# Low bits of the weights: from an OR on VectorE to an integer add on GpSimd

## Chip, cores and metric

The kernel runs on one core of one Trainium2 chip. The metric is the device time of one execution in microseconds, as the median of several runs. The names of the engines are those of the profile: PE (TensorE matmul), PEld (its weight loads), DVE (VectorE), ACT (ScalarE), POOL (GpSimd), SP (SyncE, whose queue issues every DMA of this kernel).

## What is computed

A linear attention with exponential features feeds a small feed-forward block.

```python
def phi(x):
    proj = einsum('bhsd,df->bhsf', x, w_phi)
    proj = proj - max(abs(proj), axis=-1)
    return concatenate([exp(proj), exp(-proj)], axis=-1)
q_p, k_p = phi(q), phi(k)                       # q, k, v: 8 x 8 x 576 x 64; 128 features
kv, z = einsum('bhsf,bhsd->bhfd', k_p, v), sum(k_p, axis=2)
x = (q_p @ kv) / (q_p @ z + 1e-6)               # turned to 4608 x 512
h = x @ w_in                                    # w_in 512 x 1024
solu = h * softmax(h)
ln = (solu - mean) / sqrt(var + 1e-6) * g_ln
out = ln @ w_out                                # w_out 1024 x 512
```

The weights come as 64-bit floats, and the kernel makes 32-bit floats of them on the chip, from the high word and the top three bits of the low one.

## The kernel before

The attention is cut into 16 units (batch by half of the heads), the feed-forward block into 36 tiles of 128 tokens. `op` declares some 2460 pieces of work, each with an engine, a function and what it comes after; the long tuple `SEQUENCE` lists their numbers in the order in which they are issued. Each engine works through its own pieces in that order and never passes one by, so a piece that waits holds up all that is behind it on its engine. The order is written out; nothing is decided when the program runs. A tile's buffer slot is given by the same order (`Plan.order`).

In an attention unit PE projects q and k (`qp`, `kp`, `pm`; tiles pjq, pjk, pjm), DVE takes the row maxima (m) and subtracts them (dq, dk), ACT makes the exponentials (fq, ek), PE sums them against v (`K`, `rest`, `Z`, all in tile kvT), and then makes numerators (`qo`, `qr`: num) and denominators (`qd`: den); DVE takes the reciprocal (`dc`), it goes through DRAM to be spread over partitions (rb), and POOL multiplies (`dv`: xa, xb). In a feed-forward tile ACT and POOL split x in a high and a low part (`xh`, `xl`: mxh, mxl), PE makes h from them in 24 matmuls, the softmax parts follow on DVE and ACT, the result is turned through DRAM (du, uTs), split (`uh`, `ul`), and PE makes o in 24 matmuls; ACT scales it (os), and SP stores it.

The weights come in eight pieces of 128 x 1024 pairs of 32-bit words: pieces 0 to 3 are w_in, 4 to 7 are w_out. For each piece i the steps are `wl` (SP loads it, tile wraw, 1 MB), `ws` (ACT changes the exponent of the high word in place), `wb` (two DVE steps in `w_bits`, below: the high word shifted left by 3 into tile w, then the top 3 bits of the low word or-ed in). For w_in `wh` (ACT, win_h) and `wlo` (POOL, win_l) split the result; for w_out `wg` (ACT) multiplies the gain in, `cm`, `cmp`, `cma`, `cms` make the column mean through PE and ACT, and `wc`, `woh`, `wol` subtract it and split. The raw pieces of w_in lie in the buffers of xa and xb: pieces 1 and 3 in xa, 0 and 2 in xb. So piece 3 is loaded only when piece 1 is done, piece 2 when 0 is done, and the first `dv` writes xa when piece 3 is done. The first tile's h (`moe 0 h`) comes after all four `wlo` and its own `xl`.

The profile puts nearly all instructions on L258, the line of a helper that keeps the order, so they are told apart by their tiles.

Of the kernel before, what the change touches and what calls it, by code (L numbers as in the profile page):

```python
# [8 lines left out]
U32 = mybir.dt.uint32  # L9
AF = mybir.ActivationFunctionType  # L10
ALU = mybir.AluOpType
# [14 lines left out]
KV_PE = (0, 1)  # L26
SWITCH = 165.0
# [1285 lines left out]
```

## Time and profile before

| | us |
|---|---|
| median of 3 runs (670.62 to 671.99) | 671.8 |
| the profiled execution: its own time | 670.49 |
| the profiled execution: its span, first to last instruction | 668.7 |
| PE busy | 660.4 (99%) |
| DVE busy | 491.6 (74%) |
| ACT busy | 370.3 (55%) |
| POOL busy | 394.6 (59%) |

The table's busy times are unions of spans over the whole execution. A matmul's end is modelled in the trace and lies some tenths of a microsecond behind its last column, so a PE that reads as busy may still be waiting a little; the distance from one start to the next is the better measure.

### The profile page before, as it was taken

Reading aid. Unit: us, or ns where it says so; the run is one execution under the profiler, and the core shown is the slowest. Engines: PE = TensorE matmul, PEld = TensorE weight load, DVE = VectorE, ACT = ScalarE, POOL = GpSimd, SP = SyncE. Lnnn points to the kernel's source line nnn. Section 1 sums busy time; section 2 is a strip of 40 time slices with the busy share of each in tenths; the row PEclk is TensorE's granted clock in tenths of the full one; section 3 lists DMA queues with packets and bytes.
Section 4 is the critical chain, followed back from the end, with each engine's and each line's share of the span. In section 5 each row is a group of like instructions: output and inputs, shape, how many; then the busy total and the mean of one; then the engine's idle time right before and its main releaser. Section 6 shows DMA issues by size and latency. Waiting matters only on the chain.

```text
span 668.7 us, 13163 instructions
## 1 busy us (share of the span) xinstructions
PE 660.4 (99%) x4932; PEld 493.9 (74%) x4932; DVE 491.6 (74%) x754; ACT 370.3 (55%) x717; POOL 394.6 (59%) x438
## 2 busy tenths in 40 slices
PE   8999999999999999999999999999999899999998
PEld 6776667677777777777768777787777677788887
DVE  6999888878987697797788888589675746533440
ACT  4888874566465565455664576364545563331322
POOL 0125998786675574677593955845857555554501
PEclk9999999999999999999999999999999999999999
DMA  7897888777765695887685667764874663532302
GB/s 269 303 310 230 277 215 237 220 223 243 243 192 185 217 292 191 238 260 221 191 262 158 202 210 215 263 189 124 259 218 144 213 206 92 183 113 85 104 16 80
DMA packets 131280, 135.31 MB, mean 202 GB/s; under 512 B 55568, under 2 KB 105104, under 8 KB 130704
## 3 DMA queue, kind: packets, MB, share of 16 engines
q1 hardware_dynamic: 131216, 134.46, 65.1%
q8 instruction: 39, 0.64, 0.4%
q14 instruction: 25, 0.20, 0.1%
HBM read 85.53 MB, written 48.91 MB: 201 GB/s over the span
## 4 chain that ended last, share of the span: by engine, by line
PE 86%; DVE 9%; DMA 2%; issue 1%; POOL 1%; ACT 0%; SPq 0%; DVEq 0%; POOLq 0%; ACTq 0%
PE o L258 29%; PE h L258 28%; PE kvT L258 11%; PE num L258 6%; PE pjq L258 4%; PE pjk L258 4%; PE den L258 3%; DVE m L258 2%; DVE dq L258 2%; DVE w L258 2%; DVE dk L258 1%; PE pjm L258 1%; DMA out<-os 1%; DMA rb<-d 1%; DVE dE L258 0%
## 5 line engine op out<-in xcount | busy, mean ns | idle before, releaser
L258 POOL TENSOR_TENSOR uls<-uTs,uhs 128x1024 fp32r<-128x1024 f32 x33 | 78.9, 2391 | 46.4 <-ACT uhs L258 34.9
L258 PE MATMUL o<-w_out_h,uhs 128*128 128x512 f32 x264 | 103.9, 393 | 0.0
L258 PE MATMUL o<-w_out_h,uls 128*128 128x512 f32 x264 | 102.8, 389 | 0.0
L258 PE MATMUL o<-w_out_l,uhs 128*128 128x512 f32 x264 | 102.8, 389 | 0.0
L258 ACT ACTIVATE ek<-dk 128x512 f32<-128x512 f32 (+1 forms) x160 | 88.8, 587 | 18.8 <-DVE dk L258 15.5
L258 POOL TENSOR_TENSOR zt<-ek 128x512 f32<-128x512 f32 x52 | 68.2, 1311 | 48.8 <-ACT ek L258 48.3
L258 PE MATMUL h<-win_h,mxh 128*128 128x512 f32 x288 | 91.9, 400 | 0.0
L258 ACT ACTIVATE fq<-pT 128x512 f32<-128x512 f32 (+1 forms) x140 | 74.1, 561 | 31.6 <-DMA pT<-dqd 21.3
L258 PE MATMUL h<-win_h,mxl 128*128 128x512 f32 x288 | 89.0, 390 | 0.5 <-POOL mxl L258 0.5
L258 PE MATMUL h<-win_l,mxh 128*128 128x512 f32 x288 | 89.0, 390 | 0.0
L258 DVE TENSOR_REDUCE nm<-h 128x1 f32<-128x1024 f32 x36 | 43.8, 1218 | 60.0 <-PE h L258 60.0
L258 ACT ACTIVATE eu<-h,nm 128x1024 f32<-128x1024 f32 x36 | 40.1, 1113 | 59.9 <-DVE nm L258 52.3
L258 PEld LDWEIGHTS h<-win_h,mxh 128*128 128x128 f32 x288 | 52.0, 188 | 15.4 <-issue 1.4
L258 PEld LDWEIGHTS h<-win_h,mxl 128*128 128x128 f32 x288 | 54.0, 188 | 12.4 <-POOL mxl L258 0.9
L258 PEld LDWEIGHTS h<-win_l,mxh 128*128 128x128 f32 x288 | 54.1, 188 | 11.6
L258 PE MATMUL kvT<-ek,rawv 128*64 128x256 f32 x512 | 62.0, 383 | 0.0
L258 DVE SCALAR_TENSOR_TENSOR qz<-fq,kvf,qz 128x576 f32<-128x576 f32 x46 | 44.2, 972 | 21.1 <-ACT qz L258 21.1
L258 PEld LDWEIGHTS o<-w_out_h,uhs 128*128 128x128 f32 x264 | 49.6, 188 | 11.7 <-issue 0.5
L258 PEld LDWEIGHTS o<-w_out_h,uls 128*128 128x128 f32 x264 | 49.6, 188 | 10.4
L258 PEld LDWEIGHTS o<-w_out_l,uhs 128*128 128x128 f32 x264 | 49.6, 188 | 10.0
L258 PE MATMUL num<-fq,kvf 128*64 128x448 f32 (+1 forms) x304 | 56.5, 499 | 0.0
L258 ACT ACTIVATE qz<-fq,kvf 128x576 f32<-128x576 f32 x46 | 34.6, 770 | 38.2 <-DMA kvf<-dk 38.2
(109 smaller groups left out, 1278.1 us busy)
## 6 DMA issues: line engine op xcount, KB each, us to landing
du<-ub SPq DMA_DIRECT2D x33, 512.0 KB, 3.9
uTs<-du SPq DMA_DIRECT2D x33, 512.0 KB, 5.2
rb<-d SPq DMA_DIRECT2D x64, 144.0 KB, 3.9
dqd<-dq SPq DMA_DIRECT2D x14, 640.0 KB, 4.9
pT<-dqd SPq DMA_DIRECT2D x14, 640.0 KB, 5.9
out<-os SPq DMA_DIRECT2D x35, 256.0 KB, 4.1
rawq<-in_q SPq DMA_DIRECT2D x32, 256.0 KB, 4.2
rawk<-in_k SPq DMA_DIRECT2D x32, 256.0 KB, 5.0
```

Of the source, the lines that this page charges most:

```text
L258: return self.tc.keep_in_program_order(method(*args, **kwargs))
```

## The change

The second step of `w_bits` is replaced. The three low bits are taken out of the low word in a step of their own, in place (`"lo"`), and are then added to the shifted high word by POOL as a 32-bit integer add (step 1), where before DVE did both in one instruction. For w_in (`LOW_POOL`, pieces 0 to 3) POOL also does the `"lo"` step, as a multiply and a minimum on the top byte of the word; for w_out DVE does it, as a shift. There are eight more pieces of work, and `SEQUENCE` is another order of all of them.

```diff
+LOW_POOL = (0, 1, 2, 3)
...
     def w_bits(i, step, tag):
         raw = W["raw", i]
         lo, hi = raw[:, :, 0], raw[:, :, 1]
-        if step == 0:
+        if step == "hi":
             W[i] = sb(tag, [P, DF], U32, f"w32_{i}")
             nc.vector.tensor_scalar(out=W[i], in0=hi, scalar1=3, scalar2=None, op0=ALU.logical_shift_left)
+        elif step == "lo":
+            if i in LOW_POOL:
+                nc.gpsimd.tensor_scalar(
+                    out=lo, in0=lo.bitcast(U8)[:, :, 3], scalar1=1.0 / 32, scalar2=7.484375, op0=ALU.mult, op1=ALU.min
+                )
+            else:
+                nc.vector.tensor_scalar(out=lo, in0=lo, scalar1=29, scalar2=None, op0=ALU.logical_shift_right)
         else:
-            nc.vector.scalar_tensor_tensor(
-                out=W[i], in0=lo, scalar=29, in1=W[i], op0=ALU.logical_shift_right, op1=ALU.bitwise_or
-            )
+            nc.gpsimd.tensor_tensor(out=W[i], in0=W[i], in1=lo, op=ALU.add)
...
-        op(("wb", i, 0), "vector", 600, z, w_bits, (i, 0, w_tag[i]), [("ws", i)], [(w_tag[i], T)], R4)
-        op(("wb", i, 1), "vector", 1135, z, w_bits, (i, 1, None), [("wb", i, 0)], tiles=R4 + [T])
+        op(("wb", i, "hi"), "vector", 680, z, w_bits, (i, "hi", w_tag[i]), [("ws", i)], [(w_tag[i], T)], R4)
+        op(("wb", i, "lo"), "gpsimd" if i in LOW_POOL else "vector", 680, z, w_bits, (i, "lo", None), [("wl", i)], tiles=R4)
+        op(("wb", i, 1), "gpsimd", 2400, z, w_bits, (i, 1, None), [("wb", i, "hi"), ("wb", i, "lo")], tiles=R4 + [T])
```

The numbers of the two orders, turned into names (unit or piece first), differ on every engine; on PE a piece of work moves by 0.9 places in the mean and by 9 at most. The stretches that the prediction speaks of:

```
POOL, up to the first tile's xl
  before: wlo0, dv 0 0, wlo1, dv 0 1, dv 1 0, wlo3, dv 1 1, wlo2, xl
  after:  lo1, add1, lo0, add0, wlo0, wlo1, lo3, add7, add3, add4, dv 0 0, dv 0 1, add6, lo2, wlo3, add5, add2,
          dv 1 0, dv 1 1, wlo2, qk, xl
DVE, place of a piece in its own list
  first shift of piece 7: 65 before, 53 after
SP, first pieces
  before: ql 0, wp (w_phi), kl 0, kl 2, kl 1, ql, ql 1, ql 2, vl 2, vl 0, vl 1, vl 1, ql 0, wl 1, kl 0, wl 0
  after:  ql 0, vl 1, wp (w_phi), kl 0, kl 1, kl 2, ql 1, ql, ql 2, vl 0, wl 1, vl 2, ql 0, kl 0, wl 0
ACT, round ws 1
  before: ke 2 0 0, ke 2 0 1, ke 2 1 0, ke 2 1 1, ws 1
  after:  ws 1, ke 2 0 0, ke 2 0 1, ke 2 1 0, kve 0, ke 2 1 1
PE, round unit 14's last denominators
  before: 28 h, 14 qr 0, 14 K 1, 14 qo 0, 15 kp 2, 14 Z 1, 14 qd 0
  after:  14 K 1, 14 qr 0, 14 qo 0, 28 h, 15 kp 2, 14 Z 1, 14 qd 0
PE, its end (h, t, o of the last tiles)
  before: 33 o, 35 t, 34 o, 35 o (two halves of 256 columns, each stored by itself)
  after:  35 t, 33 o, 35 o (two halves), 34 o (512 columns, stored in one piece)
```

## Rows read from the trace of the kernel before

**Rows 1.** Windows by stage: window, its length, then busy us of each engine (instructions), clock, DMA.
```profile
10.00:60.00 50.00, 50.00 (x700) 35.78 (x698) 49.27 (x86) 43.55 (x87) 8.02 (x4) 1.00 0.89 293
60.00:70.00 10.00, 9.30 (x104) 5.28 (x101) 9.97 (x20) 7.11 (x12) 9.20 (x6) 1.00 0.89 269
70.00:510.00 440.00, 439.89 (x3261) 325.39 (x3259) 355.64 (x543) 256.23 (x508) 305.47 (x325) 1.00 0.72 219
```

**Rows 2.** Waits of PE and of its weight loads, whole span: total us, times, longest.
```profile
PE den L258 <- DVE qz L258: 2.0, 1, 2.0
...
PE h L258 <- POOL mxl L258: 0.5, 1, 0.5
...
PEld cmean L258 <- ACT w L258: 1.3, 2, 0.8
```

**Rows 3.** PE's timeline in two stretches: start us, length us, what.
```profile
51.29 1.90 PE L258 MATMUL kvT<-ek,rawv 128*64 128x256 f32 x16
53.01 2.11 PE L258 MATMUL num<-fq,kvf 128*64 128x288 f32 x16
...
169.01 1.95 PE L258 MATMUL kvT<-ek,rawv 128*64 128x256 f32 x16
170.79 1.67 PE L258 MATMUL num<-fq,kvf 128*64 128x448 f32 x8
```

**Rows 4.** PE's timeline round the first tile's h.
```profile
61.42 2.63 PE L258 MATMUL cmean<-w,mean 128*32 128x512 f32 x16
...
67.92 0.70 PE L258 MATMUL h<-win_h,mxh 128*128 128x512 f32 x2
...
69.55 0.73 PE L258 MATMUL h<-win_h,mxl 128*128 128x512 f32 x2 [0.47 <-POOL mxl L258]
```

**Rows 5.** DVE's work on tile w: ns min/median/max, first and last start.
```profile
L258 DVE TENSOR_SCALAR w<-wraw x8: 643/686/920, 23.0 to 57.8; 128x1024 uint32<-128x1024 uint32 x8
L258 DVE SCALAR_TENSOR_TENSOR w<-wraw,w x8: 1216/1220/1226, 24.2 to 58.5; 128x1024 uint32<-128x1024 uint32 x8
```

**Rows 6.** Groups by form, POOL: count, busy us, mean ns, idle before.
```profile
L258 POOL TENSOR_TENSOR win_l<-w,win_h 128x1024 fp32r<-128x1024 f32 x4 | 9.5, 2376 | 29.3 <-ACT win_h L258 29.3
L258 POOL COPY pm<-pT 128x128 f32<-128x128 f32 x14 | 4.1, 292 | 0.0
```

**Rows 7.** DVE's and POOL's timelines from 40 to 65 us.
```profile
42.05 0.64 DVE L258 TENSOR_SCALAR w<-wraw 128x1024 uint32<-128x1024 uint32 x1
...
50.57 0.92 DVE L258 TENSOR_SCALAR w<-wraw 128x1024 uint32<-128x1024 uint32 x1
51.52 1.23 DVE L258 SCALAR_TENSOR_TENSOR w<-wraw,w 128x1024 uint32<-128x1024 uint32 x1
...
48.54 2.39 POOL L258 TENSOR_TENSOR win_l<-w,win_h 128x1024 fp32r<-128x1024 f32 x1
52.33 1.70 POOL L258 TENSOR_TENSOR xa<-E,rb 128x576 f32<-128x576 f32 x1 [1.40 <-DMA rb<-d]
...
64.52 1.41 POOL L258 TENSOR_TENSOR xa<-E,rb 128x576 f32<-128x576 f32 x1
```

**Rows 8.** DVE's work on tile qz, two operands in SBUF: ns min/median/max.
```profile
L258 DVE SCALAR_TENSOR_TENSOR qz<-fq,kvf,qz x46: 765/810/2372, 148.6 to 570.3; 128x576 f32<-128x576 f32 x46
```

**Rows 9.** Timeline at the start.
```profile
1.17 0.42 SPq L258 DMA_DIRECT2D wph<-in_w_phi  x1
...
4.04 2.02 PE L258 MATMUL pjq<-wph,rawq 64*128 64x128 f32 x16
```

**Rows 10.** The end: ACT's last piece, its full-width form, DMA issues after 600 us (us to landing).
```profile
665.52 0.47 ACT L258 ACTIVATE os<-o,sc 128x256 f32<-128x256 f32 x1 [2.35 <-PE o L258]
...
L258 ACT ACTIVATE os<-o,sc 128x512 f32<-128x512 f32 x35 | 24.0, 686 | 49.4 <-PE o L258 34.0 <-PE h L258 7.5 <-issue 3.7
...
out<-os SPq DMA_DIRECT2D x10, 256.0 KB, 2.1
...
out<-os SPq DMA_DIRECT2D x2, 128.0 KB, 1.7
```

More of the change, by code (lines that the diff above doesn't have):

```diff
@@ L9 @@
 U32 = mybir.dt.uint32
+U8 = mybir.dt.uint8
 AF = mybir.ActivationFunctionType
```

255 rows, old and new, of the table SEQUENCE are left out of this document.

## Prediction

> **What bounds the kernel now.** I read the windows by stage first, then PE's waits, then PE's timeline where the windows showed a gap. In the windows [rows 1] the reader should see two engines full at once up to 70 us: PE reads as busy for 50.00 of 50 us between 10 and 60, and DVE for 49.27, while POOL does 8.02 us of work. After 70 us PE stays full (439.89 of 440) and DVE falls to 355.64. So before 70 us it has to be settled which of the two sets the pace, since only DVE is relieved directly. A modelled end can hide a wait, so I took distances between starts: a group of 16 kvT matmuls takes 53.01 - 51.29 = 1.72 us in the first stage and 170.79 - 169.01 = 1.78 us in the middle, where PE is the bound beyond doubt [rows 3]. PE therefore runs as densely in the first stage as anywhere; DVE is full beside it, but PE loses almost nothing to it. What a faster first stage can give is the time that PE really loses there, not the DVE time that is saved.
>
> That loss is small and stands in two places. Round the first tile's h [rows 4], cmean, two projections and cma take 67.92 - 61.42 = 6.50 us, and 1.3 us of it is PE waiting for the last pieces of w_out from ACT [rows 2]. Between the first h matmul and the first one that needs mxl lie 69.55 - 67.92 = 1.63 us, of which 0.5 is the wait for mxl [rows 2]; four matmuls remain for 1.1. Together 1.8 us. Later there is one named wait of 2.0 us, den for qz [rows 2]. All else PE loses is spread over its changes of operation, at most a few tenths per 10 us, and a new order changes that little. So about 3.8 us is all that can be won.
>
> **The change part by part.** DVE loses eight instructions of 1.22 us and, for w_out, gains four shifts that I price like the first step, 0.69 [rows 5]: 8 x 1.22 - 4 x 0.69 = 7.0 us less. The new shift writes every second word where the first writes a packed tile; at worst it costs 1.22 like the old second step, and the saving is 4.9 us. At best it costs what the fastest first step does, 0.64: 7.2. All of it lies before 60 us [rows 5], beside a dense PE; on the path it is worth nothing by itself, only through the 1.8 us above.
>
> POOL gains eight adds and four low steps. An add reads two operands of 1024 words, as the win_l subtraction does: 2.38 us each [rows 6], 19.0 us. That an integer add costs what a float one does is not shown by any row; I keep half and double (1.2 and 4.8) as ends and take 2.38, whose shape is the same. The low step has one input of 1024: between 0.69 (DVE's shift [rows 5]) and 2.38 (two inputs on POOL); I take half of the latter, 1.2 us, which a copy of 128 elements in 0.29 us [rows 6] neither supports nor excludes. Four make 4.8 us. The Trainium skill (GPSIMD Engine Reference, section 7) counts about 1.9 cycles of 1.2 GHz per element where the step between elements is at most 8 bytes, as it is here: an estimate of 1.6 us each, by which POOL's queue would be 1.6 us longer in all; no row here shows this form.
>
> Does POOL have room? Up to the first xl its new list is 8 adds, 4 low steps, 4 wlo (2.38), 4 products (1.41 [rows 7]), one copy (0.29) and xl (at most 1.4): 19.0 + 4.8 + 9.5 + 5.6 + 0.3 + 1.4 = 40.6 us in a stage of more than 60 with 8.0 us of work up to 60 us now [rows 1]. But the list is worked in order. From the add of piece 7 on it holds 6 adds, 1 low step, 2 wlo, 4 products, the copy and xl, 14.3 + 1.2 + 4.8 + 5.6 + 0.3 + 1.4 = 27.6 us without a pause, and it can't start before DVE's shifts of piece 7. The first of these ended at 42.7 [rows 7]; it is now 12 places earlier in DVE's list, at 0.6 us a place about 35, and the second follows two places later: 36.5. So xl ends near 64 if nothing holds POOL up, and PE, as dense as now and without the 1.3 us, asks for it near 67.92 - 1.3 + 1.1 = 67.7. If piece 7 comes no earlier than now, xl ends at 42.7 + 1.3 + 27.6 = 71.6, 2.1 us later than PE has it now [rows 4]. What hides the move of the adds is thus about 3.7 us of room; if it is gone, each microsecond is one of PE's, since every h hangs on that xl.
>
> The wait that the change adds: an add waits for its shift and holds up what is queued behind it on POOL (wlo, the products, through them ACT's xh, and PE). The raw pieces are now freed by POOL, so the load of piece 3 on SP, and the loads queued behind it there, wait for POOL's add of piece 1; POOL is idle then, and I cost it at nothing, at one add (2.38) if that cover is gone.
>
> The order adds small certain costs. At the start w_phi's load is one place later on SP, behind a v piece; its issue takes 0.42 us [rows 9], and PE's first matmul at 4.04 needs it: +0.4 us, which no row hides. ACT takes ws 1 ahead of four exponentials that K 1 needs; the wait for that megabyte may show on PE: 0 to 1.5 us, I take 0.3. At the end the last store is one of 256 KB and not of 128: 2.1 against 1.7 us to land, and ACT's piece ahead of it 0.69 against 0.47 [rows 10]: +0.6 us. In the middle the wait of 2.0 us for qz may go or come back elsewhere, since PE now does tile 28's h after unit 14's K 1, qr and qo and so nearer to the denominators that waited; I take it as gone and put 0.5 us for new waits, with ends 0 and 4.
>
> Sum against the profiled execution: -1.5 (of the 1.8 us in the first stage) +0.4 +0.3 +0.6 -2.0 +0.5 = -1.7 us, 670.49 - 1.7 = 668.8. That execution lies 1.3 us under the median of the runs shown, so in terms of the median 670.1 us.
>
> **Where a rule speaks against it.** Rows show POOL and DVE in each other's way: DVE's shift took 0.92 us and not 0.69 when it started at 50.57 while POOL's win_l ran from 48.54 to 50.93, and POOL's product took 1.70 and not 1.41 when it started at 52.33 under the OR of 51.52 to 52.75 [rows 7]. The OR-like step on qz has a median of 0.81 us and a maximum of 2.37 [rows 8]. The Trainium skill (SBUF — State Buffer, section "Who interferes with whom") has the rule: a DVE instruction with two inputs in SBUF, or in a mode that uses both ports, and a GpSimd instruction lock each other out for the whole instruction. By that rule the trace agrees.
>
> **The rivals.**
>
> *The lock eats the room (slower).* The ORs, which met an idle POOL, are gone, but twelve shifts now stand beside a POOL that is full from 36 us on. Seven of them fall into the 27.6 us above; if each holds POOL for 0.6 us (one shift), xl ends 4.2 us later, near 68.5; and if each waits out half an add, 1.2 us, DVE loses 8.4 us, more than the 7.0 it was given, and piece 7's and the later shifts come no earlier than now: xl at 71 to 72. It decides from the point where xl ends after 69.5. Price: the 1.5 us not won and 2.1 to 3 us more, 670.49 - 1.7 + 1.5 + 2.5 = 672.8, in terms of the median 674.1. For it speak the rows just named; against it that DVE has less to do in front of piece 7.
>
> *The gain only moves (same).* PE is as dense as before, the 2.0 us wait comes back at another place, and the start and the end cost 1.3 us: -1.5 + 1.3 + 0.5 = +0.3, 672.1. For it speaks that PE is the bound in every row after 70 us.
>
> *It doesn't do what it says, or at another price (slower).* If an add takes 4.8 us, POOL's list grows by 14.5 us behind piece 7 and xl ends near 78, some 9 us later than now: about 680. Against it: the add reads and writes as many words as win_l's subtraction.
>
> **How the numbers follow.** Forecast 0.42, its own range 668 to 671; only moved 0.30 (671 to 673); lock 0.22 (673 to 675.5); dear add 0.06. A measurement of this kernel can tell about 0.2% from no change, 1.3 us: faster is below 670.5, slower above 673.1. Of the forecast four fifths lie below, and a little of the second case does too: faster 0.40. Same takes the rest of the forecast and most of the second case: 0.34. Slower 0.26. The range leaves out a tenth on each side: 667.5 (all of 3.8 us won, 0.4 + 0.6 us paid, 667.7, and the 1.3 us up to the median not added) to 674.4.
>
> **What would show it.** DVE's SCALAR_TENSOR_TENSOR on w is gone, and its busy time before 60 us falls below 47 us. POOL has eight adds of about 2.4 us and is busy over 30 us between 10 and 60. PE's first h matmul starts between 65.5 and 67.5, and the one for mxl follows within 1 us. PE's first matmul starts near 4.4. No wait of 2 us of den for qz. The forecast is wrong if PE's wait for mxl grows past 1 us, if the 16 matmuls of a K group in the first stage are spaced wider than now (then DVE was the bound), or if a new wait of more than 1 us stands in the middle.

## The result, and the profile after

The changed kernel takes 680.3 us, the median of 4 runs (678.2 to 682.0), against 671.2 us of before (670.1 to 672.0) on the same chip: a ratio of 1.0135, 95% interval 1.0101 to 1.0169. The forecast was 670.1 us, with a range up to 674.4; it had the wrong sign. The profiled execution took 679.79 us with a span of 678.0, so the two profiles lie 9.3 us apart.

The windows of after answer to [rows 1]; the columns are the same.

```profile
10.00:60.00 50.00, 48.91 (x656) 34.46 (x654) 48.32 (x86) 43.70 (x87) 40.59 (x15) 1.00 0.87 290
60.00:70.00 10.00, 9.47 (x138) 5.34 (x134) 7.38 (x15) 6.83 (x13) 10.00 (x6) 1.00 0.97 278
70.00:510.00 440.00, 433.98 (x3203) 318.93 (x3202) 351.01 (x538) 251.32 (x501) 300.56 (x326) 1.00 0.68 213
```

POOL has gone from 8.02 to 40.59 us of work between 10 and 60 us and is full from 60 to 70. DVE, which was to lose 7 us there, lost 0.95 in the first window. PE lost 1.09 us between 10 and 60, and 6.0 of 440 us between 70 and 510, where it had been full. PE's waits over the whole span (total us, times, longest), to be set beside [rows 2]:

```profile
PE den L261 <- DVE qz L261: 2.2, 1, 2.2
PE h L261 <- POOL mxl L261: 1.3, 2, 1.1
...
PE pjq L261 <- ACT E L261: 1.0, 1, 1.0
PE pjq L261 <- DMA wph<-in_w_phi: 0.8, 1, 0.8
PE pjq L261 <- DVE dk L261: 0.7, 1, 0.7
PE h L261 <- ACT mxh L261: 0.7, 1, 0.7
```

The wait for qz went at unit 14, as forecast, and a like one came at unit 13; the other five lines are new or longer.

**Where PE's time went.** For every step of PE I took the distance from its start to the next step's start and subtracted what a step of its kind (same function, same number of matmuls) takes in before when nothing is late (the 20th percentile of its kind there, the shorter of two where a kind has only two). The rest is what PE lost at that step. The table sums it by stage, in us, each column by the clock of its own profile. Without losses the steps take 641.5 us, and both orders hold the same steps. Rows from e1 on are the experiments below.

| profile | 0-10 | 10-75 | 75-190 | 190-215 | 215-490 | 490-530 | 530-end |
|---|---|---|---|---|---|---|---|
| before | 2.1 | 4.9 | 3.3 | 0.8 | 6.3 | 3.3 | 5.4 |
| after | 2.1 | 8.0 | 3.0 | 4.3 | 6.0 | 5.4 | 6.5 |
| e1 new order, old or | 3.9 | 7.9 | 3.1 | 4.4 | 6.2 | 6.1 | 7.1 |
| e2 old order, add | 1.4 | 16.7 | 10.5 | 1.6 | 7.0 | 0.9 | 9.5 |
| e3 low step on VectorE | 3.6 | 11.6 | 3.8 | 1.5 | 7.0 | 4.8 | 7.9 |
| e4 four forms | 3.4 | 7.3 | 3.0 | 3.1 | 6.9 | 4.8 | 8.3 |
| e5 new order, then old | 3.1 | 7.6 | 4.9 | 1.7 | 6.2 | 2.9 | 5.6 |
| e6 old order, then new | 1.4 | 5.0 | 8.4 | 1.2 | 5.8 | 4.9 | 8.0 |
| e7 one operation | 1.4 | 6.8 | 3.0 | 1.5 | 6.0 | 4.4 | 8.0 |
| e8 before, later den | 1.6 | 5.0 | 3.3 | 0.8 | 6.3 | 1.6 | 5.2 |
| e9 two pieces by the or | 3.2 | 7.6 | 3.0 | 4.5 | 5.6 | 6.0 | 6.9 |
| e10 before, new tail | 2.2 | 5.4 | 3.4 | 0.9 | 6.3 | 5.7 | 7.4 |
| e11 e8, two pieces new | 2.1 | 5.4 | 3.3 | 0.8 | 6.3 | 1.5 | 5.3 |
| e12 repairs, two by the or | 3.3 | 7.7 | 3.1 | 2.8 | 5.8 | 1.5 | 5.3 |
| e13 before, later w_phi | 1.9 | 4.3 | 4.5 | 0.8 | 6.3 | 1.4 | 5.3 |
| e14 before, new from 136 us | 1.7 | 6.2 | 7.8 | 2.2 | 7.6 | 4.7 | 8.1 |
| e15 four repairs | 1.3 | 6.8 | 3.0 | 3.2 | 6.1 | 1.6 | 5.3 |
| e17 after, gap for qz | 3.5 | 7.2 | 3.0 | 1.0 | 7.0 | 1.9 | 7.4 |

After lost 3.1 us more than before between 10 and 75 us, 3.5 between 190 and 215, 2.1 between 490 and 530 and 1.1 behind that; the others cancel to some tenths. For the first three the rows show what PE waited for.

**First stage.** POOL's and DVE's groups on the weights up to 75 us: count, busy us, mean ns, then idle time before.

```profile
L261 POOL TENSOR_TENSOR w<-w,wraw 128x1024 uint32<-128x1024 uint32 x8 | 19.7, 2472 | 0.9 <-DVE w L261 0.7
L261 POOL TENSOR_SCALAR wraw<-wraw 128x1024 uint32<-128x1024 uint8 x4 | 15.9, 3978 | 13.5 <-DMA wraw<-in_w_in 13.2
...
L261 DVE TENSOR_SCALAR w<-wraw 128x1024 uint32<-128x1024 uint32 x8 | 8.4, 1050 | 0.9 <-ACT wraw L261 0.9
L261 DVE TENSOR_SCALAR wraw<-wraw 128x1024 uint32<-128x1024 uint32 x4 | 3.9, 975 | 0.0
```

The add came at 2.47 us, as priced. The low step came at 3.98 us; I had taken 1.2, with 2.38 as the upper end. And DVE's twelve shifts take 12.3 us in place of the 8.3 that twelve undisturbed ones would. POOL's list (start us, length) then runs from 35.8 us to mxl with 0.7 us of pause, and PE gets to the first h before mxl is there. First, DVE's second shift of piece 7, which the list waits for:

```profile
38.44 0.64 DVE L261 TENSOR_SCALAR wraw<-wraw 128x1024 uint32<-128x1024 uint32 x1
```
```profile
35.82 4.29 POOL L261 TENSOR_SCALAR wraw<-wraw 128x1024 uint32<-128x1024 uint8 x1
40.19 2.43 POOL L261 TENSOR_TENSOR w<-w,wraw 128x1024 uint32<-128x1024 uint32 x1
...
54.69 3.88 POOL L261 TENSOR_SCALAR wraw<-wraw 128x1024 uint32<-128x1024 uint8 x1
...
71.36 1.28 POOL L261 TENSOR_TENSOR mxl<-xa,mxh 128x512 fp32r<-128x512 f32 x1
```
```profile
70.35 0.73 PE L261 MATMUL h<-win_h,mxh 128*128 128x512 f32 x2
70.93 0.62 PE L261 MATMUL h<-win_l,mxh 128*128 128x512 f32 x2
72.70 0.73 PE L261 MATMUL h<-win_h,mxl 128*128 128x512 f32 x2 [1.14 <-POOL mxl L261]
```

In [rows 4] the first of these began at 67.92, and the one that needs mxl at 69.55. The wait for mxl is 0.7 us longer than before, so most of the 3.1 us was lost ahead of it. At 46.93 PE stands 0.7 us for DVE's dk, which comes behind two shifts of 1.52 and 1.18 us beside POOL's adds. The two steps of cmean take 4.4 us and not 2.7, since ACT has w later: it waits 3.2 us for POOL's add. The weight loads show it, after first, then before:

```profile
PEld cmean L261 <- ACT w L261: 2.8, 4, 1.4
```
```profile
PEld cmean L258 <- ACT w L258: 1.3, 2, 0.8
```

**At 500 us.** DVE's work on tile qz (ns min/median/max, first and last start) and, below it, POOL's timeline beside it:

```profile
L261 DVE SCALAR_TENSOR_TENSOR qz<-fq,kvf,qz x2: 807/3158/5509, 498.9 to 499.6; 128x576 f32<-128x576 f32 x2
```
```profile
499.24 1.58 POOL L261 TENSOR_TENSOR zacc<-zacc,ek 64x512 f32<-64x512 f32 x1
500.78 1.41 POOL L261 TENSOR_TENSOR xa<-E,rb 128x576 f32<-128x576 f32 x1
502.14 2.35 POOL L261 TENSOR_TENSOR uls<-uTs,uhs 128x1024 fp32r<-128x1024 f32 x1
504.58 0.58 POOL L261 TENSOR_SCALAR sa<-sm 128x1 f32<-128x1 f32 x1
```

The second qz begins at 499.60, takes 5.51 us instead of 0.81, and ends at 505.1: 0.6 us behind the last of three POOL operations that follow each other without a gap. PE's den stands 2.2 us for it.

**From 190 to 215 us.** PE waits for ACT's E, and ACT had waited for pT (unit 6's projected queries, turned through DRAM) before the exponentials that stand ahead of this E. SP issues the load of pT 9 us later than before. Before, its order is dk (the store of unit 5's keys times values), pT, kvf (dk loaded again); after, pT comes behind kvf and four other loads, and kvf is issued only when dk has landed. PE's row and the two waits of after, then SP's rows of before and of after:

```profile
194.10 2.05 PE L261 MATMUL pjq<-wph,rawq 64*128 64x128 f32 x30 [0.97 <-ACT E L261]
...
ACT fq L261 <- DMA pT<-dqd: 3.7, 1, 3.7
...
SPq L261 <- DMA dk<-kvs: 3.8, 1, 3.8
```
```profile
174.42 0.33 SPq L258 DMA_DIRECT2D dk<-kvs  x1
...
175.64 0.42 SPq L258 DMA_DIRECT2D pT<-dqd  x1
...
176.71 0.61 SPq L258 DMA_DIRECT2D kvf<-dk  x1
```
```profile
177.40 0.32 SPq L261 DMA_DIRECT2D dk<-kvs  x1
181.59 0.60 SPq L261 DMA_DIRECT2D kvf<-dk  x1
...
184.91 0.38 SPq L261 DMA_DIRECT2D pT<-dqd  x1
```

From the issue of dk to that of kvf pass 4.2 us in after. Among the experiments with this order of SP they are 2.0 to 2.2 us in e3, e6 and e17, where the stage loses 1.0 to 1.5 us, and 3.4 to 4.1 in e1, e4, e7, e9, e12, e14 and e15, where it loses 1.5 to 4.5. In e2 and e5, with before's order of SP there, they are 4.1 and 4.3, and the stage loses 1.6 and 1.7. No run moves the load of pT alone, so that its place is the cause is argued from these rows, not tested.

### The profile page after: what moved, and what is told of

Read it like the earlier page. It is cut to its first block, busy times and chain, and to the rows that moved or that the text cites. A ratio compares the mean times of both kernels' runs of the same rounds, so it can differ in the third digit from the quotient of the medians.

```text
span 678.0 us, 13213 instructions
## 1 busy us (share of the span) xinstructions
PE 663.1 (98%) x4932; PEld 493.8 (73%) x4932; DVE 488.8 (72%) x750; ACT 368.6 (54%) x717; POOL 428.0 (63%) x450
## 4 chain that ended last, share of the span: by engine, by line
PE 86%; DMA 4%; POOL 3%; DVE 3%; issue 2%; ACT 1%; SPq 1%; POOLq 0%; ACTq 0%
PE h L261 29%; PE o L261 28%; PE kvT L261 11%; PE num L261 6%; PE pjk L261 4%; PE pjq L261 4%; DMA rb<-d 3%; PE den L261 2%; POOL xa L261 1%; SPq L261 1%; PE pjm L261 1%; DVE qz L261 1%; POOL w L261 1%; POOL wraw L261 1%; DVE m L261 1%
## 5 line engine op out<-in xcount | busy, mean ns | idle before, releaser
L261 PEld LDWEIGHTS o<-w_out_h,uls 128*128 128x128 f32 x264 | 49.5, 188 | 10.5
L261 POOL TENSOR_TENSOR xa<-E,rb 128x576 f32<-128x576 f32 (+1 forms) x32 | 29.3, 919 | 43.6 <-DMA rb<-d 34.0
```

Of the source, the lines that this page charges most:

```text
L261: return self.tc.keep_in_program_order(method(*args, **kwargs))
```

## The experiments

Ratios are to the kernel before on the same chip. Its median read 669.1 to 671.2 us beside the various experiments, so kernels are compared by their ratios. The expectations say TensorE, VectorE, ScalarE and GpSimd for PE, DVE, ACT and POOL.

**Order and arithmetic apart.** e1 keeps the order of after, puts the or back and leaves the low step out (its cut in part):

```
-            nc.gpsimd.tensor_tensor(out=W[i], in0=W[i], in1=lo, op=ALU.add)
+            nc.vector.scalar_tensor_tensor(
+                out=W[i], in0=lo, scalar=29, in1=W[i], op0=ALU.logical_shift_right, op1=ALU.bitwise_or)
```

> The new order with the old arithmetic: the low bits are or-ed in on VectorE (1.22 us each, eight times) in the place of the add, the low step is left out. Theory 1, two causes: GpSimd's low step of 3.9 us makes its queue late by about 3 us at the first h, and the new order by itself brings the waits at 192 to 213 us, at 502 us and at the end (some 6 us). Then here the second h matmul of the first routing starts at 71 to 72 us (71.50 before, 74.63 after), the waits at 192 and 502 stay, and the time is 675 to 677.5. Theory 2, all from GpSimd: the late waits follow from the late and locked first stage; then they go with it and the time is 670.5 to 672.5. Theory 3, all from the order: the first stage is late here too and the time is 679 to 681.

Measured: 683.2 us, 1.0194 [1.0165, 1.0223], no faster than after (the intervals just touch). Theory 3 came nearest, and even its time was too low. Without any add or low step on POOL the new order loses 7.9 us between 10 and 75 us, now because DVE is late (PE's steps that need its dq at 50 us and its dk at 69 us lose 2.0 us each), and it loses as much at 190 and at 500 us as after does. So those two places don't need the new arithmetic. Of what e1's profile loses over after's, 1.8 us lie in the first 10 us, which the edit doesn't touch. After its wait of 1.7 us for E the granted clock read 0.50, the lower level, from 198.0 to 201.3 us; in after it read 1.00 from 190 to 215.

e2 is the converse: before's order, with low step and add in the place of the or.

> The old order with the new arithmetic: at the old place of the or stand the low step (GpSimd for the four pieces of w_in, 3.9 us each; VectorE for the four of w_out, 0.7 us each) and the add on GpSimd (2.4 us each). Theory 1, two causes: only the first stage is late, by 3 to 6 us, since 35 us of new GpSimd work stand in an order made without them; nothing new waits after 75 us, and the time is 674 to 677. Theory 2, all from GpSimd: the late first stage brings waits of its own later on, 678 to 682. Theory 3, all from the order: 670.5 to 672.

Measured: 691.8 us, 1.0321 [1.0290, 1.0352]. The size was missed by far: POOL's new work in an order made without it holds up the products xa behind it on its queue (ACT's E waits 8.7 us for xa, and PE 6.3 us for that E at 62 us). Neither half of the change is cheaper alone than the whole.

**The low step.** e3 gives all eight low steps to VectorE:

```
-LOW_POOL = (0, 1, 2, 3)
+LOW_POOL = ()
```

> After with the low step of all eight pieces on VectorE (as a shift, 0.69 us each alone), the adds on GpSimd. GpSimd is freed of 15.9 us before 60 us, VectorE gets 4 x 0.7 = 2.8 us. Theory 1: the second h matmul starts at 71 to 72.5 us, mxl is no longer the last it waits for, the waits at 192 and 502 stay, and the time is 675 to 678. Theory 2: 671 to 673, without those waits. Theory 3: 679 to 681.

Measured: 686.0 us, 1.0242 [1.0209, 1.0276], above every theory: 7 us over after, although POOL is rid of 15.9 us and DVE was given a nominal 2.8. DVE's and POOL's timelines of e3 show why:

```profile
27.73 2.94 DVE L261 TENSOR_SCALAR w<-wraw 128x1024 uint32<-128x1024 uint32 x1
...
31.46 2.78 DVE L261 TENSOR_SCALAR wraw<-wraw 128x1024 uint32<-128x1024 uint32 x1
34.16 0.68 DVE L261 TENSOR_REDUCE m<-pjq 128x4 f32<-128x512 f32 x1
```
```profile
27.70 2.42 POOL L261 TENSOR_TENSOR w<-w,wraw 128x1024 uint32<-128x1024 uint32 x1 [5.91 <-DVE wraw L261]
31.31 2.38 POOL L261 TENSOR_TENSOR win_l<-w,win_h 128x1024 fp32r<-128x1024 f32 x1 [1.19 <-ACT win_h L261]
```

Both shifts, 0.69 us when nothing holds them, start just behind a POOL operation of two inputs and end 0.55 us after it. The sixteen shifts take 19.4 us together instead of 11, and PE stands 3.4 us for DVE's dk in this stretch. The rival of the prediction that named this lock had the mechanism.

e4 measures forms of the low step, one for each piece.

```
+ piece 0: in0=lo.bitcast(U8)[:, :, 3], scalar1=1.0 / 32,   op0=mult
+ piece 1: in0=lo,                      scalar1=2.0**-29,   op0=mult, op1=min
+ piece 2: in0=lo.bitcast(U16)[:, :, 1], scalar1=1.0 / 8192, op0=mult, op1=min
+ piece 3: as after, out=lo.bitcast(I32)
```

> After with four forms of GpSimd's low step, one for each piece of w_in, all exact: piece 0 the byte times 1/32 without the min; piece 1 the whole 32-bit word in place of the byte; piece 2 the upper 16 bits in place of the byte; piece 3 the byte with a signed 32-bit result. After's own four took 3.86 to 4.29 us. If the second operation costs it, piece 0 takes 2.4 us or less and the others 3.9; if reading single bytes costs it, pieces 1 and 2 take 2.4 us; if the conversion to an unsigned word does, piece 3 takes 2.4; if the loop of a GpSimd tensor_scalar with conversion costs it in any form, all four take 3.8 to 4.3. The time is 678 to 682 whichever holds, unless two or more forms are cheap (676 to 679).

The groups of e4's low steps by form (the first column after the bar is busy us):

```profile
L263 POOL TENSOR_SCALAR wraw<-wraw 128x1024 int32<-128x1024 uint8 x1 | 4.1, 4122 | 0.1
L263 POOL TENSOR_SCALAR wraw<-wraw 128x1024 uint32<-128x1024 uint16 x1 | 3.9, 3883 | 0.1
L263 POOL TENSOR_SCALAR wraw<-wraw 128x1024 uint32<-128x1024 uint32 x1 | 3.9, 3877 | 12.8 <-DMA wraw<-in_w_in 12.8
L263 POOL TENSOR_SCALAR wraw<-wraw 128x1024 uint32<-128x1024 uint8 x1 | 3.0, 3012 | 0.1
```

Neither the width of what is read nor the sign of the result makes it cheaper (piece 3 took 4.29 in after). The second operation costs 0.87 us; what is left, 3.0 us, is still more than an add with two inputs. The time, one run, was 681.2.

e7 takes the cheapest form for all four pieces (the min changes no value).

```
-scalar1=1.0 / 32, scalar2=7.484375, op0=ALU.mult, op1=ALU.min
+scalar1=1.0 / 32, scalar2=None, op0=ALU.mult
```

> After with the low step of GpSimd as one operation (byte times 1/32, the min left out, the value is the same): 3.0 us in place of 3.9 for each of the four pieces. Of these 0.9 us, two lie in GpSimd's unbroken list from 36 us to mxl at 72.6 us. If that list sets the time of the first h: mxl comes 1.7 us earlier, the wait for it (1.1 us) falls under 0.2 us, and the time is 1 to 1.5 us under that of after, 678.5 to 679.5. If VectorE, the locks or the loads set it: 679.5 to 681, as after.

Measured: 676.8 us, 1.0104 [1.0075, 1.0133], 2 us under after by the ratios, whose intervals overlap. The table gives 1.2 us of it to 10 to 75 us, as expected, and the rest to other stages. But mxl is still waited for 0.9 us: POOL now stands 0.6 and 0.9 us for DVE's shifts at the head of its list, where after had one such wait of 0.7.

e9 goes on from e7 and takes the two late pieces off POOL altogether.

```
-LOW_POOL = (0, 1, 2, 3)
+LOW_POOL = (0, 1)
+OR = (2, 3)
...
+        elif i in OR:
+            nc.vector.scalar_tensor_tensor(
+                out=W[i], in0=lo, scalar=29, in1=W[i], op0=ALU.logical_shift_right, op1=ALU.bitwise_or
+            )
```

> The kernel with one operation in the low step, and for the two late pieces of w_in (3 and 2) the old or on VectorE in the place of low step and add. GpSimd's list from 35 us to mxl loses 2 x (3.0 + 2.4) = 10.9 us, VectorE gets 2 x 1.2 us. If that list sets the first h: mxl is no longer waited for, the second h matmul comes at 70.5 to 71.5 us (72.70 with one operation, 74.64 after, 71.50 before), and the time is 674 to 676 (676.8 with one operation). If the locks or the loads set it: 676 to 678 and the second h no earlier than 72.3.

Measured: 680.9 us, 1.0172 [1.0141, 1.0204]: 4.6 us worse than e7, not 1.5 better. The wait for mxl is gone (0.2 us), and yet the loss between 10 and 75 us rose from 6.8 to 7.6 us: now PE waits for DVE's dk (1.4 and 1.1 us), and one shift took 2.90 us under two adds. More of the difference lies in the start (1.8 us) and at 190 to 215 (3.0, with the granted clock at 0.50 from 196.5 to 199.8 us after a wait of 1.8 for E), stages that this edit doesn't touch and that vary between profiles of the new order; so the 4.6 us are not the price of this edit alone. My theory that POOL's list alone sets the first h falls with this run. POOL and DVE share the limit; work taken from POOL came back on DVE, with shifts held under adds.

**The later stretches.** e5 and e6 join the orders at the h of the third tile: new then old with all new arithmetic, and old then new with the or.

> After up to the 416th step of its order (through the h of the third routing tile, 88 us into the profile of after), with all its new arithmetic; from there the order of before. If the loss of after behind 88 us (3.5 us at 190 to 215, 2.2 at 490 to 530, 0.7 at the end) lies in the new order of those stretches alone, it goes: 673 to 675, the wait at 192 gone, one den wait of 2 us near 523, an end of 3.4 us. If it follows from the late first stage, it stays: 678 to 681.

> Before up to the 408th step of its order (through the h of the third routing tile, 85 us into the profile of before), with the old or on VectorE; from there the order of after. If the new order of the later stretches brings its waits by itself: 673.5 to 676, with waits at about 189 to 210, at 499, and an end of 4.3 us. If they follow from the late first stage: 668.5 to 670.5.

Measured: 675.9 us, 1.0086 [1.0058, 1.0115], and 679.6 us, 1.0140 [1.0106, 1.0174]. Behind 490 us e5 lost 8.6 us, as before (8.6), and e6 12.9, as after (11.9) or more: that loss goes with the order of that stretch. The totals were missed because a join costs something of its own. The steps round it come in a sequence that neither order has; e6 lost 5 us between 88 and 96 us, part of it with the granted clock at 0.50 (93.3 to 96.6).

e10 puts the join where the two orders hold almost the same steps, at 450 us, with all arithmetic old.

> Before through the first half of the 22nd routing tile's h (450 us), then the order of after; all arithmetic old. The stretches behind 490 us lost 3.3 to 4.7 us more than in before in all five profiles with the new tail, and nothing in the one with the old tail behind the new first stage. If that belongs to the order of the tail: 672.8 to 674.5, with the den wait at 497 and an end of 4.2 us. If it needs what came before: 669.5 to 671.

Measured: 674.15 us, 1.0072 [1.0045, 1.0099], as expected: 4.8 us (3.0 to 6.6) for the new order behind 450 us alone. Its qz takes 5.52 us beside the same three POOL operations as in after.

e17 breaks that run of three in after and changes nothing else: four small POOL operations that have long had their input go ahead of uls.

```
  POOL  before the edit: zh 0, dv, ul 22, sc 19        after it: zh 0, dv, sc 19, ul 22
```

> After with one step of GpSimd's order moved: the four small operations of a layer norm (128x1, 1.5 us, their input there since 485 us) stand ahead of uls, so that zacc (1.58 us), xa (1.41) and uls (2.35) are no longer one unbroken run from 499.24 to 504.49 us. In after VectorE's second qz began at 499.60, took 5.51 us in place of 0.81 and ended 0.6 us behind uls; TensorE's den stood 2.21 us for it. If VectorE is held by GpSimd's unbroken run: qz ends 0.6 us behind xa, takes 2.9 to 3.4 us, the wait for it falls under 0.3 us and the time is 2 to 4.5 us under that of after (676 to 678). If qz was held by something else: 5.5 us again, and 680.

Measured: 675.5 us, 1.0095 [1.0062, 1.0128]. POOL's timeline, and DVE's with its two qz in one row:

```profile
497.58 1.59 POOL L259 TENSOR_TENSOR zacc<-zacc,ek 64x512 f32<-64x512 f32 x1
499.14 1.41 POOL L259 TENSOR_TENSOR xa<-E,rb 128x576 f32<-128x576 f32 x1
500.63 0.58 POOL L259 TENSOR_SCALAR sa<-sm 128x1 f32<-128x1 f32 x1
...
502.36 2.40 POOL L259 TENSOR_TENSOR uls<-uTs,uhs 128x1024 fp32r<-128x1024 f32 x1
```
```profile
497.23 3.93 DVE L259 SCALAR_TENSOR_TENSOR qz<-fq,kvf,qz 128x576 f32<-128x576 f32 x2
501.09 1.21 DVE L259 TENSOR_TENSOR eu<-h,eu 128x1024 f32<-128x1024 f32 x1
```

The pair takes 3.93 us and not 6.24, ends 0.6 us behind xa, and den waits no more: the loss between 490 and 530 us falls from 5.4 to 1.9. That settles what held qz. In the total, e17 is 2.7 us below after by the ratios, whose intervals overlap.

e14 puts the old order and the or up to 136 us ahead of the new order.

> Before up to 136 us (the key projection of the sixth unit), from there the order of after to the end; all arithmetic old, no lock from 32-bit adds, first stage on time. If the stretch at 190 to 215 us has its loss (2 to 3.7 us in five profiles, 0.3 to 0.9 in four) from the new order alone: 676 to 678, 2 to 3.5 us over the kernel that has only the new tail (674.15), with TensorE waiting near 187 us for the bank that ScalarE's E frees. If it needs the late first stage: 673.5 to 675, as that kernel.

Measured: 681.6 us, 1.0180 [1.0153, 1.0206], unusable for its question: the join cost 4.5 us between 144 and 157 us. The step of PE that waits for ACT's E at 192 us in after loses 1.0 us here, at 195, with a first stage in time, so it doesn't need a late one. Its size varies from execution to execution: e17 has after's order and arithmetic up to 499 us and lost 1.0 us between 190 and 215 where after lost 4.3. The landing of dk goes with it (2.0 us from dk's issue to kvf's in e17, 4.2 in after); what makes that store slow or fast stays open.

**The start.** e13 moves one load in before.

```
-  SP: ql 0, wp (w_phi), kl 0, ...
+  SP: ql 0, vl 1, wp (w_phi), kl 0, ...
```

> Before with one transfer moved: the values of the first unit's middle tile (64 KB) are loaded ahead of w_phi, as in after. The first projection starts at 4.03 to 4.04 us in the profiles with the old start and at 4.25 to 5.34 us in those with the new. If the place of w_phi is the cause: 4.7 to 5.2 us, and 0.7 to 1.2 us over before (669.8 to 670.5). If not: 4.0 to 4.3 us and the time of before.

Measured: 670.3 us, 1.0009 [0.9994, 1.0025]. PE's first projection, in e13 and in after, beside 4.04 in [rows 9]:

```profile
4.80 1.16 PE L256 MATMUL pjq<-wph,rawq 64*128 64x128 f32 x16 [0.70 <-DMA wph<-in_w_phi]
```
```profile
4.91 1.16 PE L261 MATMUL pjq<-wph,rawq 64*128 64x128 f32 x16 [0.81 <-DMA wph<-in_w_phi]
```

The place of w_phi makes PE's first step 0.76 us later, but its 16 matmuls take 1.16 us and not 2.02, so the next step begins at 5.77 us (5.87 in after, 5.89 before): in these two profiles nothing is lost by 10 us. In e1, e3, e4, e5, e9, e12 and e17, with w_phi in the same place, the late first step took 2.08 us, and the stage lost 3.1 to 3.9 us; why, no run shows. In e13's time, 0.6 us, the place of w_phi can't be told from nothing. And in e13's profile den doesn't wait for qz at 521 us (the stage lost 1.4 us, not 3.3), although PE's order is that of before: the wait in [rows 2] varies, too.

**Can it be mended, and does any version beat before?** e12 and e15 put the repairs together. e12: one operation, pieces 3 and 2 by the or, the old order from 453 us, the later den of e8. e15: one operation on all four pieces, w_phi in its old place, the old order from 453 us, the later den.

> All repairs on after at once: low step in one operation, pieces 3 and 2 by the or, from 453 us on the order of before, with the later den. If the parts add up: 680.3 - 3.5 - 1.5 - 3.5 - 1.6 = 670.2, so 669 to 671.5. If the new order between 80 and 450 us costs something of its own that the tail hid: 672 to 675.

> After with four repairs: the low step in one operation, w_phi in its old place, from 453 us on the order of before, the later den. From the single runs: 676.8 (one operation) - 3.4 to 4.7 (tail) - 1.6 (den) - 0.9 (w_phi) = 669.6 to 670.9. If the new arithmetic in its own order is worth something once the rest is as before, it comes under the kernel with the later den alone (668.5); if the stretch at 190 to 215 comes back, 671.5 to 674.

Measured: 675.7 us, 1.0089 [1.0057, 1.0121], and 671.8 us, 1.0025 [1.0010, 1.0041]. e12 carries the price of e9. e15 comes within 0.25% of before, yet 3.3 us over e8, which has its tail: 1.8 us of that lie in 10 to 75 us and 2.4 in 190 to 215. So this version gains nothing. The 2.4 us go with SP's order, not with the arithmetic; what the new arithmetic is worth without that, no run shows.

e8 is before with one PE step moved over the den that waits in [rows 2]:

```
-  PE: ..., 14 Z 1, 14 qd 0 (den), 25 o 0, 25 o 1
+  PE: ..., 14 Z 1, 25 o 0, 14 qd 0 (den), 25 o 1
```

> Before with one step of TensorE's order moved: the o of the 25th routing tile's first half (2.7 us, its input long there) goes ahead of the den matmuls that stand 2.0 us for VectorE's qz at 521 us. If the wait is only covered: it falls under 0.2 us and the time is 1.5 to 2 us under before (ratio 0.997 to 0.998). If the later den makes its own followers late (dn, the division, its two DMA, xa, the h of that tile): the same wait turns up within 30 us and the time is that of before.

Measured: 668.45 us, 0.9976 [0.9959, 0.9992]: 1.6 us below before, and so below both kernels. PE's timeline: no wait is left at den.

```profile
520.08 0.43 PE L256 MATMUL kvT<-zacc,ones 128*32 128x128 f32 x8
520.44 0.50 PE L256 MATMUL o<-w_out_h,uhs 128*128 128x512 f32 x1
...
523.39 0.69 PE L256 MATMUL den<-qz,ones 128*32 128x288 f32 x8
```

e11 adds to e8 the new arithmetic where POOL has nothing else to do, on the first two pieces of w_in, in the old order.

```
+LOW_POOL = (0, 1)
+OR = (2, 3, 4, 5, 6, 7)
```

> The kernel with the later den (668.5), and in its old order the two first pieces of w_in (1 and 0) by GpSimd: low step in one operation right behind the load, then the add; GpSimd has nothing else to do there (its first win_l starts at 48 us in before). The other six keep the or. VectorE is freed of 2 x 1.2 us before 25 us. If VectorE's load in the first stage costs TensorE time: 667 to 668. If TensorE is dense there whatever VectorE is freed of: 668 to 669. If the longer step (2.4 against 1.2 us) and the locks make win_h late: 669 to 671.

Measured: 668.9 us, 0.9984 [0.9962, 1.0006], as e8. Relieving DVE of 2.4 us before 25 us changed nothing for PE.

## Why the prediction was wrong, step by step

By the table, the terms of the sum came out like this: the first stage +3.1 us where -1.5 stood; the middle (the wait for qz and new waits) +5.6 where -2.0 + 0.5 stood; the start 0 and not +0.4; the end +1.1 and not +0.6; the other stages lost 0.6 less. Two steps failed: that DVE and POOL had room for the change in the first stage, and that the new order is all but free in the middle.

- **PE is the bound and DVE's relief is worth little by itself: held.** (The 1.3 us at cmean were read from waits of the weight loads; by the distances PE lost 0.75 there and 0.7 in the two projections behind, so the size was about right.) The steps take 641.5 us of the span without losses, and e11 shows relief of DVE that buys nothing. What I missed is the other side: DVE had little time to give away, so what holds it can become PE's loss, as at 46.93 and at 502.95 us.
- **DVE saves 7.0 us: failed.** Its work on the weights fell from 15.45 us to 12.30. Eight ORs went and four shifts came, as priced, but the twelve shifts were held for 4 us in all (the longest 1.99 us at 26.67, under POOL's add from 25.68 to 28.10).
- **The add at 2.38 us: held** (2.47). The "dear add" rival is out.
- **The low step at 1.2 us, at most 2.38: the mis-sized term.** 3.86 to 4.29 us, four times 2.8 us more on POOL's queue, one of them in the list that ends in mxl and one right in front of it. I bounded it by an operation with as many words and more inputs, and nothing in the trace had its form, a GpSimd tensor_scalar with conversion. The estimate from the Trainium skill (GPSIMD Engine Reference, section 7), 1.6 us, was also far too low; the measurement decides.
- **Room of 3.7 us ahead of the first xl: used up twice over.** The list from the add of piece 7 on, 27.6 us from 36.5, started at 40.19 and ended at 72.6 instead of 64: 8.5 us late, past the 69.5 that I had named as the turning point. DVE's second shift of piece 7 ended at 39.08 and not at 36.5, which is 2.6 us of it, and piece 3's low step, right in front of the list, held it another 1.1. In the list piece 2's low step took 3.88 - 1.2 = 2.7 us more; a pause of 0.7 and the longer xa, adds and win_l make up the rest.
- **The lock: named as a rival at 0.22, for 674.1.** The mechanism was right and its places were too few. I counted it only in the first stage. The 5.5 us qz at 500 us, which e17 shows to be the same thing, and e3 tell that it can strike wherever the order puts POOL's long operations beside a DVE instruction of this kind. The rule of the Trainium skill (SBUF — State Buffer, section "Who interferes with whom"), by which the first of the two to issue keeps the other out for its whole instruction, agrees with these rows as far as it goes: they show DVE kept out for a whole run of instructions.
- **The wait for qz taken as gone (-2.0), new waits +0.5 with ends 0 and 4: failed.** One like it came at 502.95 for 2.2 us, with the clock's fall behind it (below), and 190 to 215 us added 3.5 in this execution. Together the two stages lost 5.6 us more than before, so even the end of 4 was too low (-2.0 + 4 = 2.0). A new order of some 2,460 steps is no small edit where PE is full in every stage, and I had not followed the queues of DVE, POOL and SP there. e10 prices its tail alone at 4.8 us.
- **w_phi +0.4:** the first step came 0.87 us later in after, 0.76 in e13, and in both the next step was in time again. **The end +0.6:** beyond the matmuls of the last o the span lasts 4.3 us and not 3.4, +0.9. **ws 1 ahead of the exponentials +0.3:** no wait of PE names it.
- **The list of signs worked as a warning.** The first h was to start between 65.5 and 67.5 us with mxl within 1 us; it started at 70.35 with mxl 2.35 us later. DVE was to fall below 47 us before 60; it read 48.32.

## What to carry to other kernels

Moving work from a full engine to an idle one pays only if the bounding engine loses time to the full one, and the idle engine's queue is in order, so its new list has to be timed up to the next operation that the bounding engine needs (the issuing order of the DMA queue is such a list, too), and an operation in a form that no row shows has to be priced high. Where two engines lock each other out, work moved between them can cost more than its own length; look for long unbroken runs of one beside the other, anywhere in the kernel. And an order found for one set of costs is part of the kernel: judge a new order by its own waits, stage by stage, apart from the edit that it comes with.

## What the runs showed of the hardware that I had not expected

- GpSimd's tensor_scalar on 1024 words with an integer result takes 3.9 to 4.3 us with two operations, whether it reads bytes, halves or words, and 3.0 with one (reading bytes), while its 32-bit integer add of two tensors takes 2.4, as the fp32 subtraction does.
- VectorE isn't let in between GpSimd operations that follow each other without a gap: one qz was held over three (5.51 us), and with a run of two it took 3.21; it ended 0.6 us behind the run each time.
- After the 2.2 us wait for qz TensorE's granted clock was at its lower level, 1.2 GHz, for nearly all of 3.5 us (0.52 in the mean), and the 12 matmuls of h took 4.30 us, not 2.72. The windows of after:

```profile
506.00:509.50 3.50, 3.11 (x7) 2.48 (x8) 3.43 (x7) 0.96 (x3) 2.32 (x3) 0.52 0.17 61
509.50:512.00 2.50, 2.50 (x12) 2.08 (x11) 1.08 (x2) 0.00 (x0) 0.00 (x0) 0.99 0.91 322
```

In before the clock stayed at 1.00 after its wait of 2.0 us at 521; there TensorE went on to its o matmuls at once, while in after it stood another 0.5 us for eu. What decided it, these runs don't show. e10, with the same wait, has the same fall (0.52 from 501 to 504.5 us).
